# The channel weight of a mixer kernel loaded in full rows, and the first batches' steps placed anew

## The chip, the cores and the metric

The kernel runs on one core of one Trainium2 chip. The time is the device time of one execution in microseconds (us). The kernel before was run three times: 288.15, 288.61 and 289.21 us, so the median is 288.61 us. One execution of its own was profiled.

## The reference

For each of 8 batches and 8 heads (576 positions, 64 columns) the first part is attention under a mask: heads 0 to 3 see the last 32 positions, heads 4 to 7 see every fourth of the last 128. The second part is a mixer over the heads' joined output x (576 x 512):

```
scores = where(mask, q @ k.T / 8, -1e9);  attn = softmax(scores);  x = attn @ v   (heads side by side)
h = relu(x.T @ w_tok1) @ w_tok2          # w_tok1 576x256, w_tok2 256x576
u = x + h.T
out = u + relu(u @ w_ch1) @ w_ch2        # w_ch1 512x1536, w_ch2 1536x512
```

Inputs and output are float32; the kernel computes in fp16 with float32 sums.

## The kernel before

**Engines.** TensorE (PE) does all products and some transposes. ScalarE (ACT) and VectorE (DVE) empty its PSUM banks: exponentials, the scaling by the row sums, relu, the sums with x and u, and copies of transposed tiles. GpSimd (POOL) casts the loaded q, k and v to fp16, masks scores, and issues the DMAs of the weights, which cast from float32 to fp16 on the way. SyncE (SP) issues the loads of q, k and v, the DMA transposes of later batches and the stores.

**Order.** The program is written in the order in which each engine runs it; no scheduler changes that. Batch 0's attention, its h1 (the token product, `emit_h1`) and its u run first, alone (lines 888 to 970). Then, for each batch b, `gen_main(b)` (lines 747 to 814) yields pieces of the channel product: 12 blocks `gp_b_mb` of four 512-column matmuls each, over the four 128-row blocks cb of w_ch1, each followed by a relu into `gt`; then the second product `yp_b_s`, in pieces of six 256-column matmuls, whose sum with u is stored. `interleave` (line 816) runs this main line and counts its time by the number that each piece yields, and puts between its pieces the steps of the following batches, sorted by the times written for them. So during the main line of batch b the attention of batch b+1 is finished (`value_steps`, av), h1 and u of batch b+1 are made (`mix_steps`), and the scores of batch b+2 are begun. The lists with the times stand in lines 1006 to 1042.

**Weights.** w_ch1 lies in three tiles `w3[0..2]`, each of all 512 rows and 512 of the 1536 columns, so each row of a tile is 2 KB of the input. Its loads are issued by POOL: `load_w3(0)` (line 878) after the four casts of v's plain heads, `load_w3(1)` (line 881) after the two casts of `l_vd`, `load_w3(2)` (line 984) between the first casts of batch 1. Channel block mb reads tile mb // 4. Behind `load_w3(1)` on POOL stands the cast of `l_vx` into `vt` (line 882), which the value products of heads 4 to 7 of batch 0 read (line 611).

**Banks.** PSUM has eight banks: three called main, which gp and yp take in turn; two called sc (scores); three called fl for the rest. A bank is written anew when the instruction that read it last is done.

**Batch 1.** For each pair hp of heads, `transposes` turns c_q and c_k on PE; DVE or ACT copies the turned q into `qz` (line 102 or 100) and DVE the turned k into `kt` (line 314). The score matmuls (line 425, after line 423, which writes the mask into the bank) read both. POOL casts all of c_q and c_k of batch 1. Batch 2 has its own turning (`bare_steps`, k copied in line 385) and scores in pairs of half-height matmuls (line 510). u is turned by `emit_uT` (names tpu; line 673 and others), which takes fl banks.

Of the kernel before, what the change touches and what calls it, by code (L numbers as in the profile page):

```python
# [68 lines left out]
def kernel(  # L69
# [16 lines left out]
    def fixed(name, shape, dtype=FP16):  # L86
        return sb.tile(shape, dtype, tag=name, bufs=1, name=name)
# [16 lines left out]
    def relu(eng, out, in_):  # L104
        if eng is nc.scalar:
            nc.scalar.activation(out=out, in_=in_, func=AF.Relu)  # L106
        else:
            eng.tensor_scalar_max(out=out, in0=in_, scalar1=0.0)  # L108
# [510 lines left out]
    def emit_h1(b, jb, half, t):  # L619
        x = xn[b]  # L620
        j = slice(jb, DTOK, 2)
        c = slice(256 * half, 256 * half + 256)
        w = w1p if half else w1n
        p = bank("fl", 3, f"h1p_{b}_{jb}_{half}")[:, 0:256]
        nc.tensor.matmul(out=p, lhsT=w1t[b % 2][:, j], rhs=x[:, 4, c], start=True, stop=False)  # L625
        for s in range(4):
            nc.tensor.matmul(out=p, lhsT=w[:, s, j], rhs=x[:, s, c], start=False, stop=(s == 3))  # L627
        relu(nc.vector if jb and (b == 1 or (b == 0 and half)) else nc.scalar, t[:, c], p)

    def emit_u(b, s, h1):  # L630
        p = bank("fl", 3, f"up_{b}_{s}")
# [67 lines left out]
    def score_steps(b, t0, dt, offs=(0.0, 0.7, 2.0), places=None, lag=0.0):  # L699

        steps = []
        if twinned(b):
            for g in range(2):
                f = scores_twin(b, g)
                at = t0 + g * dt
                steps.append((at, 0.86, lambda f=f: next(f)))
                for i in range(7 if g else 9):
                    steps.append((at + lag * (i + 1), 0.0, lambda f=f: next(f)))
            return steps
        for hp in range(4):  # L710
            at, at_s = places[hp] if places else (t0 + hp * dt, t0 + hp * dt + dt)
            for nm in ("q", "k"):
                steps.append((at + 0.9 * (nm == "k"), 0.28, lambda nm=nm, hp=hp: transposes(b, nm, hp)))
# [33 lines left out]
    def gen_main(b):  # L747
# [2 lines left out]
        m0 = 640 * odd  # L750

        def w3_block(cb, mb):
            return w3[mb // 4][:, cb, mb % 4:512:4]

        def gp_tails(g):
            p = bank("main", 3, f"gt_{b}_{g}")
            for i in range(4):
                for cb in order:
# [3 lines left out]
            relu(nc.scalar, gta[:, 4 * g:4 * g + 4, 512:640],  # L762
                 p.rearrange("p (i t) -> p i t", t=128))

        for mb in range(NMB):
            p = bank("main", 3, f"gp_{b}_{mb}")
            for i, cb in enumerate(order):
                nc.tensor.matmul(out=p, lhsT=w3_block(cb, mb), rhs=uT[(b, cb)][0], start=(i == 0), stop=(i == 3))  # L768
                if i == 1:
                    yield 0.43  # L770
            relu(nc.vector if (mb % 2 == 1 if b == 0 else mb % 4 != 3 if b == 1 else mb in (1, 5)) else nc.scalar, gta[:, mb, m0:m0 + 512], p)
            yield 0.43
            if odd and mb in (3, 6, 9):
                gp_tails(mb // 3 - 1)
                yield 0.9
# [80 lines left out]
        nc.gpsimd.tensor_copy(out=t, in_=src)  # L856

    def load_w3(i):
        c = slice(512 * i, 512 * i + 512)
        nc.gpsimd.dma_start(out=w3[i], in_=moe_w_ch1[:, c].rearrange("(x p) c -> p x c", p=128))  # L860

    cast_qk(0, "q", 0, nc.scalar)
    cast_qk(0, "k", 0, nc.vector)
# [11 lines left out]
    for s in range(4):  # L875
        cast_vn(0, s, nc.gpsimd)
    nc.gpsimd.dma_start(out=w2a[:, :, 0:S], in_=moe_w_tok2.rearrange("(p j) t -> p j t", j=2))
    load_w3(0)
    cast_vd(0, 0, nc.gpsimd)
    cast_vd(0, 2, nc.gpsimd)  # L880
    load_w3(1)
    cast_vx(0, nc.gpsimd)
# [96 lines left out]
            load_qk(1, nm, h0, h0 + 4, nc.sync)  # L979
    load_v(1)  # L980
    casts1 = cast_steps(1)
    for i in (0, 1):
        casts1[i]()
    load_w3(2)
    for i in (2, 3, 4, 5, 7, 6, 8, 9, 10, 11):
        casts1[i]()
    for i in range(3):
        nc.gpsimd.dma_start(
# [17 lines left out]
    for b in range(B):  # L1006
        steps = []
        if b == 0:
            steps += score_steps(1, 0, 0, (0.0, 0.7, 1.5),
                                 ((3.0, 5.2), (4.4, 7.0), (7.2, 9.6), (8.6, 11.4)))  # L1010
            va = value_steps(1, 13.4, 0.7)
            steps += va[:4] + [(p + 0.3, c, f) for p, c, f in va[4:]]
            steps += mix_steps(1, 18.0, 20.6, 22.6, 31.4, 1.1)
            steps += at(24.0, 0.3, cast_steps(2))
            bare = bare_steps(2)
            scores2 = score_steps(2, 29.6, 4.4, lag=0.25)
            scores2 = sorted(scores2, key=lambda st: st[0])
            steps += [(t, 0.25, f) for t, f in zip((25.2, 25.9, 27.0, 27.6, 28.2, 34.8, 35.2, 35.6, 36.0), bare)]
            steps += scores2[:10]
            steps += at(34.0, 0.0, [lambda: emit_loads_qk(3)])  # L1020
        elif b == 1:
            va = value_steps(2, 0.0, 1.0)
            steps += [(0.8 + 0.4 * i, c, f) for i, (_, c, f) in enumerate(scores2[10:])]
            steps += [(t, c, f) for t, (_, c, f) in zip((2.2, 3.0, 4.8, 5.6, 8.2, 9.0, 10.4, 11.2), va)]
            steps += mix_steps(2, 7.0, 12.4, 14.6, 24.4, 1.0, 5.6, 0.8)
# [6 lines left out]
            steps += at(11.0, 0.9, dma_steps(3)) + at(17.0, 0.4, place_steps(3))  # L1032
        else:
            late = 2.4 * (b % 2)
            if b + 1 < B:
                steps += value_steps(b + 1, 0.4, 0.95) + mix_steps(b + 1, 5.4, 9.0, 11.4, 22.4 + late)
# [36 lines left out]
```

## Time and profile before

| | us |
|---|---|
| median of three runs | 288.61 |
| the profiled execution, its own time | 289.66 |
| span of that execution, first to last instruction | 287.8 |
| outside the span | 1.9 |
| PE busy | 276.8 |
| DVE, ACT, POOL busy | 132.1, 134.0, 163.0 |
| mean granted TensorE clock | 1.00 |

All times below are us from the start of the span. In a timeline row stand the start, the busy time, the engine, the line, the operation, the names written and read, the shape, and how many instructions the row merges; in brackets stands for how long the engine was idle before it and what ended that. The busy time of a matmul contains its way through the array, so matmuls that follow each other overlap: the time from one start to the next is what each costs. A wait shorter than that way leaves no bracket and shows only in the starts.

Batch 0's channel product starts at 28.47 and batch 1's at 69.24.

### The profile page before, as it was taken

To read this page: it belongs to the slowest core of one execution; us is meant where nothing else is said; L and a number is where in the kernel's file an instruction comes from. 1 tells how busy PE (TensorE), PEld (TensorE's weight loads), DVE (VectorE), ACT (ScalarE), POOL (GpSimd) and SP (SyncE) were. 2 spreads that over 40 slices of the span, in tenths; PEclk is the share of its full clock that TensorE was granted. 3 is DMA by queue.
4 is the path that set the end of the run, shared out by engine and by line. 5 is a ranking of instruction groups with operands and counts; after the bars stand their busy time and mean duration, and the time that the engine had idled before them with its cause. 6 is when DMAs were issued, how large, how long until landed. Compare 5 with 4: busy or idle time off the path is not lost.

```text
span 287.8 us, 6995 instructions
## 1 busy us (share of the span) xinstructions
PE 276.8 (96%) x2838; PEld 210.9 (73%) x2838; DVE 132.1 (46%) x278; ACT 134.0 (47%) x265; POOL 163.0 (57%) x221
## 2 busy tenths in 40 slices
PE   5879999999999999999999999999999999999995
PEld 2777676888766886698776976797766966886594
DVE  7747658446764236414640164416440274421022
ACT  2854673263543804574447615482546534225500
POOL 6961860478865799449970999279952930000000
PEclk9999999999999999999999999999999999999999
DMA  7999999993999998979888978299974210431023
GB/s 218 263 211 218 283 225 207 320 218 82 328 210 192 264 264 230 139 164 350 226 159 182 330 224 186 57 219 329 193 150 95 85 64 2 91 112 37 0 76 108
DMA packets 105551, 52.63 MB, mean 183 GB/s; under 512 B 73872, under 2 KB 104464, under 8 KB 105520
## 3 DMA queue, kind: packets, MB, share of 16 engines
q1 hardware_dynamic: 101280, 47.07, 67.0%
q0 software_dynamic: 2640, 3.94, 8.0%
q10 hardware_dynamic: 1600, 1.18, 1.4%
q8 instruction: 22, 0.36, 0.6%
q14 instruction: 9, 0.07, 0.1%
HBM read 37.07 MB, written 9.44 MB: 162 GB/s over the span
## 4 chain that ended last, share of the span: by engine, by line
PE 80%; DMA 8%; DVE 3%; POOL 3%; issue 2%; ACT 2%; ACTq 1%; SPq 0%; POOLq 0%; DVEq 0%
PE yp L787 29%; PE gp L768 24%; DMA l_vd<-in_v_dram 4%; PE h1p L627 4%; PE yp L807 3%; DMA l_k<-in_k_dram 3%; PE up L639 3%; PE sc L510 3%; PE gt L759 3%; DVE xn L112 1%; DMA kr<-c_k 1%; PE h1p L625 1%; PE av L608 1%; PE up L650 1%; PE av L603 1%
## 5 line engine op out<-in xcount | busy, mean ns | idle before, releaser
L787 PE MATMUL yp<-w,gt 128*128 128x256 f16 x756 | 87.1, 273 | 0.0
L787 PEld LDWEIGHTS <-gt 128*128 128x128 f16 x768 | 78.6, 106 | 6.5
L106 ACT ACTIVATE gt<-gp 128x512 f16<-128x512 f32 x69 | 41.2, 597 | 76.3 <-PE gp L768 76.0
L768 PE MATMUL gp<-utd,w 128*128 128x512 f16 x144 | 54.7, 380 | 0.0
L768 PE MATMUL gp<-utm,w 128*128 128x512 f16 x144 | 54.6, 379 | 0.0
L768 PEld LDWEIGHTS <-w 128*128 128x128 f16 x384 | 39.2, 114 | 20.3 <-issue 0.5
L797 DVE TENSOR_TENSOR o<-yp,u 128x512 f32<-128x512 f32 x31 | 21.4, 691 | 63.1 <-PE yp L787 58.5
L112 POOL TENSOR_TENSOR attp<-attp,const 128x1280 f16<-128x1280 f16 x12 | 31.4, 2616 | 27.5 <-ACT attp L534 27.4
L112 DVE TENSOR_TENSOR xn<-av,rec 128x320 f16<-128x320 f32 x64 | 31.4, 491 | 2.2
L112 POOL TENSOR_TENSOR attd<-attd,const 128x1024 f16<-128x1024 f16 x12 | 25.3, 2132 | 1.6 <-ACT attd L534 1.6
L768 PE MATMUL gp<-uT,w 128*128 128x512 f16 x96 | 25.8, 379 | 0.0
L108 DVE TENSOR_SCALAR gt<-gp 128x512 f16<-128x512 f32 x27 | 18.5, 686 | 13.6 <-PE gp L768 13.1
L645 DVE TENSOR_TENSOR u<-up,xn 128x512 f16<-128x512 f32 x26 | 17.9, 690 | 7.5 <-PE up L639 7.5
L534 ACT ACTIVATE attp<-sc 128x480 f16<-128x480 f32 (+1 forms) x36 | 16.1, 536 | 7.4 <-PE sc L510 7.4
L102 POOL CAST c_k<-l_k 128x512 f16<-128x512 f32 x29 | 18.0, 628 | 1.9 <-DMA l_k<-in_k_dram 1.7
L102 POOL CAST c_q<-l_q 128x512 f16<-128x512 f32 x27 | 16.8, 629 | 3.1 <-DMA l_q<-in_q_dram 3.1
L616 DVE RECIPROCAL rec<-av 128x5 f32<-128x5 f32 x64 | 12.2, 190 | 13.8 <-PE av L613 13.7
L106 ACT ACTIVATE h<-h1p 128x256 f16<-128x256 f32 x29 | 11.1, 384 | 14.5 <-PE h1p L627 14.1
L399 POOL COPY kt<-kr 128x512 f16<-128x512 f16 x10 | 10.7, 1075 | 9.0 <-DMA kr<-c_k 9.0
L697 ACT COPY utd<-utm 128x512 f16<-128x512 f16 x12 | 12.8, 1135 | 4.1 <-DMA utm<-u 4.1
L102 POOL CAST vv<-l_vn 128x256 f16<-128x256 f32 x32 | 12.0, 420 | 4.3 <-DMA l_vn<-in_v_dram 4.1
L112 POOL TENSOR_TENSOR attt<-attt,const 128x512 f16<-128x512 f16 x12 | 14.0, 1165 | 0.0
(147 smaller groups left out, 459.9 us busy)
## 6 DMA issues: line engine op xcount, KB each, us to landing
out_dram<-o SPq DMA_DIRECT2D x72, 128.0 KB, 3.1
l_q<-in_q_dram SPq DMA_DIRECT2D x15, 512.0 KB, 7.2
l_k<-in_k_dram SPq DMA_DIRECT2D x14, 512.0 KB, 7.1
l_vn<-in_v_dram SPq DMA_DIRECT2D x32, 128.0 KB, 6.6
l_vd<-in_v_dram SPq DMA_DIRECT2D x16, 256.0 KB, 4.6
w<-in_moe_w_ch_dram POOLq DMA_DIRECT2D x6, 512.0 KB, 7.6
lt<-in_q_dram SPq DMA_DIRECT2D x8, 128.0 KB, 4.6
l_vt<-in_v_dram SPq DMA_DIRECT2D x8, 128.0 KB, 4.9
```

Source lines behind the costliest of these rows:

```text
L102: eng.tensor_copy(out=out, in_=in_)
L106: nc.scalar.activation(out=out, in_=in_, func=AF.Relu)
L108: eng.tensor_scalar_max(out=out, in0=in_, scalar1=0.0)
L112: eng.tensor_tensor(out=out, in0=x, in1=y, op=ALU.mult)
L534: nc.scalar.activation(out=out, in_=in_, func=AF.Exp, scale=0.125)
L616: nc.vector.reciprocal(out=rec[:, :, 0], in_=av[:, :, 64])
L627: nc.tensor.matmul(out=p, lhsT=w[:, s, j], rhs=x[:, s, c], start=False, stop=(s == 3))
L645: nc.vector.tensor_tensor(out=u16(b, s), in0=blocks4(p), in1=blocks4(xn[b][:, s]), op=ALU.add)
L697: nc.scalar.copy(out=natural(uTd[:, cb - 2]), in_=uTm[i][:, cb].rearrange("p r m -> p m r"))
L768: nc.tensor.matmul(out=p, lhsT=w3_block(cb, mb), rhs=uT[(b, cb)][0], start=(i == 0), stop=(i == 3))
L787: nc.tensor.matmul(out=p[:, c], lhsT=gta[:, mb, a0:m0 + 512:4] if half else gta[:, mb, a0:a0 + 128], rhs=w4[mb][:, c], start=(mb == 0), st ...
L797: nc.vector.tensor_tensor(out=blocks4(o32), in0=blocks4(p), in1=u16(b, s), op=ALU.add)
```

## The change

- w_ch1 lies in two tiles of full rows: `w3[0]` holds row blocks cb 0 to 2 with all 1536 columns (6 KB of the input a row), `w3[1]` block cb 3. There are two loads; the third is gone from its place among batch 1's casts. On POOL the first load is issued after the first cast of `l_vd`, not before it.
- In batch 0, gp_0, gp_1 and gp_2 first run their matmuls over cb 0 to 2 in the three main banks; then their fourth matmuls run one after the other.
- c_q of batch 1's pairs 0 and 1 is cast by ACT, not POOL.
- Batch 1's transposes of q and of k have times of their own, and with their scores, values, h1 and u and with batch 2's first steps stand 1.0 to 1.6 later in the list of batch 0's main line.
- DVE no longer does the relu of gp_7, gp_9 and gp_11 of batch 0, and of batch 1's h1; ACT does.
- In batch 1's main line, h1's second half of batch 2 stands at 13.0, not 12.4, u at 15.1, not 14.6, and the placing of batch 3's turned k at 16.4, not 17.0. In odd main lines from 3 on h1 stands 0.4 later.

```
-    w3 = [fixed(f"w3_{i}", [128, 4, 512]) for i in range(3)]
+    w3 = [fixed(f"w3_{i}", [128, 3 - 2 * i, DCH]) for i in range(2)]
...
+            return w3[cb // 3][:, cb % 3, c0 + mb % 4:c0 + 512:4]
...
+        if b == 0:
+            for mb in range(3):
+                first.append(bank("main", 3, f"gp_{b}_{mb}"))
+                for cb in range(3):
+                    nc.tensor.matmul(out=first[mb], lhsT=w3_block(cb, mb), rhs=uT[(b, cb)][0], start=(cb == 0), stop=False)
+                yield 0.65
...
-                                 ((3.0, 5.2), (4.4, 7.0), (7.2, 9.6), (8.6, 11.4)))
-            va = value_steps(1, 13.4, 0.7)
+                                 ((4.2, 5.9, 7.1), (5.0, 6.6, 8.9), (7.8, 9.2, 11.2), (9.0, 10.2, 13.0)))
+            va = value_steps(1, 14.8, 0.7)
```

POOL in the program's start, before. `l_vd` and `l_vx` are loaded v, `vv` and `vt` their casts, `w_0` and `w_1` tiles of w_ch1.

```order
L877 DMA w_81<-in_moe_w_tok_dram 128x2x576
L860 DMA w_0_84<-in_moe_w_ch_dram 128x4x512
L102 CAST vv_69<-l_vd_123 128x4x2x64 x2
L860 DMA w_1_85<-in_moe_w_ch_dram 128x4x512
L102 CAST vt_71<-l_vx_124 128x4x64
```

POOL at the same place, now.

```order
L887 DMA w_81<-in_moe_w_tok_dram 128x2x576
L102 CAST vv_69<-l_vd_122 128x4x2x64
L869 DMA w_0_84<-in_moe_w_ch_dram 128x3x1536
L102 CAST vv_69<-l_vd_122 128x4x2x64
L869 DMA w_1_85<-in_moe_w_ch_dram 128x1536
L102 CAST vt_71<-l_vx_123 128x4x64
```

The first load moved behind one cast; the second still stands ahead of the cast into `vt`.

DVE in batch 0's main line, before. `tp_q_1` is the bank with the turned q of pair 1, and so on.

```order
L108 TENSOR_SCALAR gt<-gp_3_677 128x512
L314 COPY kt<-tp_k_0_695 128x512
L102 COPY qz<-tp_q_1_701 64x576 x2
L102 COPY kt<-tp_q_1_701 128x64
L314 COPY kt<-tp_k_1_724 128x512
L108 TENSOR_SCALAR gt<-gp_5_713 128x512
```

DVE at the same place, now.

```order
L108 TENSOR_SCALAR gt<-gp_3_673 128x512
L102 COPY qz<-tp_q_1_699 64x576 x2
L102 COPY kt<-tp_q_1_699 128x64
L108 TENSOR_SCALAR gt<-gp_5_696 128x512
L314 COPY kt<-tp_k_0_714 128x512
L314 COPY kt<-tp_k_1_723 128x512
```

The copy of pair 0's k, which the first scores of batch 1 read, moved behind the copies of pair 1's q and the relu of gp_5. On PE there stand between gp_4 and those scores, now: tp_q_0, half of gp_5, tp_q_1, the rest of gp_5, half of gp_6, tp_k_0, the rest of gp_6, tp_k_1.

DVE ahead of batch 2's first scores, before. `u_1` is u of batch 1, `o_0_1` an output tile, `kt` from `tp_k_1` the turned k of pair 1 of batch 2.

```order
L645 TENSOR_TENSOR u_1_1065<-up_3_1124,xn_886 128x4x128
L385 COPY kt<-tp_k_0_1131 128x512
L385 COPY kt<-tp_k_1_1153 128x512
L797 TENSOR_TENSOR o_0_1_1100<-yp_1_1099,u_0_499 128x512
L102 COPY uT_0_1240<-tpu_0_1239 128x640
```

DVE at the same place, now.

```order
L645 TENSOR_TENSOR u_1_1072<-up_3_1134,xn_893 128x4x128
L385 COPY kt<-tp_k_0_1142 128x512
L807 TENSOR_TENSOR o_0_1_1077<-yp_1_1076,u_0_498 128x512
L385 COPY kt<-tp_k_1_1167 128x512
L102 COPY uT_0_1244<-tpu_0_1243 128x640
```

The sum for the output tile moved ahead of the copy of k. On PE one piece of yp stands between these scores and the first turning of u (tpu_2), where two stood.

More of the change, by code (lines that the diff above doesn't have):

```diff
@@ L627, in emit_h1 @@
             nc.tensor.matmul(out=p, lhsT=w[:, s, j], rhs=x[:, s, c], start=False, stop=(s == 3))
-        relu(nc.vector if jb and (b == 1 or (b == 0 and half)) else nc.scalar, t[:, c], p)
+        relu(nc.vector if jb and half and b == 0 else nc.scalar, t[:, c], p)
     def emit_u(b, s, h1):
@@ L710, in score_steps @@
         for hp in range(4):
-            at, at_s = places[hp] if places else (t0 + hp * dt, t0 + hp * dt + dt)
-            for nm in ("q", "k"):
-                steps.append((at + 0.9 * (nm == "k"), 0.28, lambda nm=nm, hp=hp: transposes(b, nm, hp)))
+            at_q, at_k, at_s = places[hp] if places else (t0 + hp * dt, t0 + hp * dt + 0.9, t0 + hp * dt + dt)
+            for nm, at in (("q", at_q), ("k", at_k)):
+                steps.append((at, 0.28, lambda nm=nm, hp=hp: transposes(b, nm, hp)))
             g = (scores_plain if hp < 2 else scores_dil)(b, hp)
@@ L763, in gp_tails @@
                  p.rearrange("p (i t) -> p i t", t=128))
+        first = []
+        if b == 0:
[4 more added lines that the diff above has]
+                yield 0.65
         for mb in range(NMB):
-            p = bank("main", 3, f"gp_{b}_{mb}")
+            p = first[mb] if mb < len(first) else bank("main", 3, f"gp_{b}_{mb}")
             for i, cb in enumerate(order):
+                if mb < len(first) and i < 3:
+                    continue
                 nc.tensor.matmul(out=p, lhsT=w3_block(cb, mb), rhs=uT[(b, cb)][0], start=(i == 0), stop=(i == 3))
@@ L770, in gen_main @@
                     yield 0.43
-            relu(nc.vector if (mb % 2 == 1 if b == 0 else mb % 4 != 3 if b == 1 else mb in (1, 5)) else nc.scalar, gta[:, mb, m0:m0 + 512], p)
-            yield 0.43
+            relu(nc.vector if (mb % 2 == 1 and mb < 7 if b == 0 else mb % 4 != 3 if b == 1 else mb in (1, 5)) else nc.scalar, gta[:, mb, m0:m0 + 512], p)
+            yield 0.22 if mb < len(first) else 0.43
             if odd and mb in (3, 6, 9):
@@ L858, in load_w3 @@
     def load_w3(i):
-        c = slice(512 * i, 512 * i + 512)
-        nc.gpsimd.dma_start(out=w3[i], in_=moe_w_ch1[:, c].rearrange("(x p) c -> p x c", p=128))
+        nc.gpsimd.dma_start(
+            out=w3[i], in_=moe_w_ch1[384 * i:384 + 128 * i, :].rearrange("(x p) c -> p x c", p=128))
     cast_qk(0, "q", 0, nc.scalar)
@@ L877 @@
     nc.gpsimd.dma_start(out=w2a[:, :, 0:S], in_=moe_w_tok2.rearrange("(p j) t -> p j t", j=2))
+    cast_vd(0, 0, nc.gpsimd)
     load_w3(0)
-    cast_vd(0, 0, nc.gpsimd)
     cast_vd(0, 2, nc.gpsimd)
@@ L981 @@
     casts1 = cast_steps(1)
[L982 to L985, printed above, removed]
+    for i in (0, 2, 4, 5, 7, 6, 8, 9, 10, 11):
         casts1[i]()
@@ L1031 @@
             steps += at(6.0, 0.0, [lambda: load_v(3)]) + at(20.8, 0.9, load_steps(4))
-            steps += at(11.0, 0.9, dma_steps(3)) + at(17.0, 0.4, place_steps(3))
+            steps += at(11.0, 0.9, dma_steps(3)) + at(16.4, 0.4, place_steps(3))
         else:
@@ L1035 @@
             if b + 1 < B:
-                steps += value_steps(b + 1, 0.4, 0.95) + mix_steps(b + 1, 5.4, 9.0, 11.4, 22.4 + late)
+                steps += value_steps(b + 1, 0.4, 0.95) + mix_steps(b + 1, 5.4 + late / 6, 9.0, 11.4, 22.4 + late)
             if b + 2 < B:
```

15 lines of the change are left out of this document (8 added, 7 removed).

## Prediction

> **What bounds the kernel now.** The page of the profile first:
>
> ```profile
> span 287.8 us, 6995 instructions
> ...
> PE 276.8 (96%) x2838; PEld 210.9 (73%) x2838; DVE 132.1 (46%) x278; ACT 134.0 (47%) x265; POOL 163.0 (57%) x221
> ```
>
> PE is busy for 96% of the span. So time is made of PE's work, which the change leaves as it is (the same matmuls in another order), and of PE's waits. The page's own time was 289.66, 1.86 us more than the span; I sum against it and carry the difference to the median of the runs, 288.61, which is 1.05 lower. Next the list of what PE waited for, total, times, longest:
>
> ```profile
> PE av L611 <- POOL vt L102: 1.2, 1, 1.2
> ...
> PE h1p L625 <- DVE xn L112: 0.4, 1, 0.4
> ```
>
> Apart from the launch the first of these is PE's longest wait: the value products of batch 0 wait 1.2 us for `vt`. The others are small, so all that there is to win lies in that row and in stalls of about half a us; what there is to lose is any new wait on PE.
>
> **The front, POOL.** The timeline of POOL:
>
> ```profile
> 15.31 0.77 POOL L860 DMA_DIRECT2D w<-in_moe_w_ch_dram  x1
> 16.55 0.62 POOL L102 CAST vv<-l_vd 128x512 f16<-128x512 f32 x1 [0.46 <-DMA l_vd<-in_v_dram]
> 19.08 0.63 POOL L102 CAST vv<-l_vd 128x512 f16<-128x512 f32 x1 [1.91 <-DMA l_vd<-in_v_dram]
> 19.65 0.74 POOL L860 DMA_DIRECT2D w<-in_moe_w_ch_dram  x1
> 20.38 0.42 POOL L102 CAST vt<-l_vx 128x256 f16<-128x256 f32 x1
> ...
> 30.21 0.61 POOL L102 CAST c_q<-l_q 128x512 f16<-128x512 f32 x1 [0.80 <-DMA l_q<-in_q_dram]
> ...
> 39.20 1.61 POOL L988 DMA_DIRECT2D w<-in_moe_w_ch_dram  x3
> ```
>
> The weight's second load (19.65) takes 0.74 and stands between the second `l_vd` cast and the `vt` cast. It has 512 rows of 2 KB now and will have 128 of 6 KB; the loads at 39.20, 128 rows each, take 1.61 for three, 0.54 for one. So `vt` comes 0.20 earlier, and with it PE's start of the channel product: -0.20. The first load now goes into the 1.91 us in which POOL waits for `l_vd` at 17.2, at no cost to anyone. The bounds: 0, if an issue costs the same whatever its rows; -1.2, the whole wait, if `l_vd` lands sooner because the weight is not issued ahead of it. I take -0.20: the row 39.20 has just these 128 rows, and before 17.2 little of the weight can have moved. [...]
>
> **Does the weight arrive?** What POOL's DMA queue moved (packets, MB, share of the engines) from 19 to 24, all w_ch1 in packets of 1 KB, with the issue's time to landing, and from 42 to 48, w_ch2 in packets of 4 KB:
>
> ```profile
> q0 software_dynamic: 782, 0.79, 104.5%
> ...
> w<-in_moe_w_ch_dram POOLq DMA_DIRECT2D x1, 512.0 KB, 6.9
> ```
> ```profile
> q0 software_dynamic: 336, 1.25, 104.4%
> ```
>
> 0.79 MB in 5 us are 158 GB/s, 1.25 MB in 6 us 208. Rows of 3 KB in fp16 lie nearer to the second; I take 190. The first tile, 1.18 MB, then needs 6.2 us and the second, 0.39 MB, 2.1. Of the 6.9 to landing 3.3 were the moving of 0.52 MB and 3.6 the rest; so, issued at 17.2, the first is there at 27.0 and the second at 29.1. PE asks at 28.3 and 30.4 (below). The cover is 1.3; beyond it each us costs one.
>
> **Batch 0's channel product.** PE, and ACT with one later row:
>
> ```profile
> 28.47 3.48 PE L768 MATMUL gp<-uT,w 128*128 128x512 f16 x14
> 31.79 0.39 PE L309 MATMUL tp_q<-const,c_q 128*128 128x128 f16 x4
> ...
> 32.07 1.03 PE L768 MATMUL gp<-uT,w 128*128 128x512 f16 x4
> 32.93 0.39 PE L309 MATMUL tp_k<-const,c_k 128*128 128x128 f16 x4
> ```
> ```profile
> 28.45 0.59 ACT L100 COPY uT<-tpu 128x512 f16<-128x512 f16 x1 [0.38 <-PE tpu L673]
> 29.83 0.60 ACT L106 ACTIVATE gt<-gp 128x512 f16<-128x512 f32 x1 [0.79 <-PE gp L768]
> ...
> 81.26 1.13 ACT L100 CAST c_q<-l_q 128x512 f16<-128x512 f32 x2
> ```
>
> Four channel matmuls cost 32.93 - 32.07 = 0.86, so 0.215 each; five turnings 0.28. On the clock of before: nine matmuls from 28.47, with the short wait for the turned u that ACT ends at 29.04, reach 30.6. There gp_0's fourth starts; it is out 0.38 later (1.03 less three steps), and ACT's relu takes 0.60, so the bank is free at 31.6. PE has run the three fourths by 31.25 and waits for that bank with gp_3: +0.4 (0.3 to 0.5). No work covers it; in the order of before two whole blocks lie between. The wait of 0.1 for the last turned u goes.
>
> Then gp_3 to 32.5, gp_4 to 33.4, tp_q_0, half of gp_5, tp_q_1 to 34.4, and so on to the first scores at 36.1. The casts of c_q on ACT (1.13 for two, last row) follow the relu of gp_2 and end at about 33.3; tp_q_0 asks at 33.4. They start no sooner than q has landed, in the row of POOL at 30.21; the weight's longer load may push that back by 2, to 32.2, just in time.
>
> **The late copy.** DVE at this place:
>
> ```profile
> 32.70 0.69 DVE L108 TENSOR_SCALAR gt<-gp 128x512 f16<-128x512 f32 x1 [1.31 <-PE gp L768]
> 33.35 0.69 DVE L314 COPY kt<-tp_k 128x512 f16<-128x512 f16 x1
> 33.96 1.51 DVE L102 COPY qz<-tp_q 64x576 f16<-64x576 f16 x2
> 35.49 0.23 DVE L102 COPY kt<-tp_q 128x64 f16<-128x64 f16 x1
> 35.63 0.68 DVE L314 COPY kt<-tp_k 128x512 f16<-128x512 f16 x1
> ```
>
> Now tp_q_1 is out at 34.6. From there the two copies of q cost 1.53 (33.96 to 35.49), the small one 0.14, the relu of gp_5 0.60 to 0.65 (rows 32.70 and 35.63, to the next start), and the copy of pair 0's k 0.69: it ends at 37.5. PE reaches the first score that reads it at 36.2, and all of PE's later work is queued behind that matmul. I take +1.3. Lower bound 0.3: tp_k_0 leaves PE only at 35.5, so even a copy that nothing delayed would end at 36.4. Upper bound 1.7, if ACT's casts come late.
>
> Batch 1's scores, and its values with h1, by the view of windows (length, PE busy):
>
> ```profile
> 34.30:43.10 8.80, 8.46 (x127) 7.02 (x126) 5.90 (x13) 6.59 (x15) 6.33 (x14) 1.00 1.16 220
> 43.10:53.20 10.10, 9.90 (x119) 7.13 (x116) 7.47 (x21) 2.63 (x6) 0.91 (x3) 1.00 1.07 238
> ```
>
> PE idles 0.34 and 0.20 there. I leave that as it is: DVE has fewer relus, but u's first product now stands right behind h1's last, whose relu nothing covers. 0, between -0.5 and +0.3.
>
> **Before batch 2's scores.** PE, ACT and DVE:
>
> ```profile
> 61.19 1.50 PE L787 MATMUL yp<-w,gt 128*128 128x256 f16 x12
> 62.65 0.38 PE L673 MATMUL tpu<-const,u 128*128 128x128 f16 x4
> ...
> 69.24 0.59 PE L768 MATMUL gp<-uT,w 128*128 128x512 f16 x2
> ```
> ```profile
> 62.19 0.40 ACT L534 ACTIVATE attt<-sc 128x256 f16<-128x256 f32 x1
> ```
> ```profile
> 59.89 0.69 DVE L385 COPY kt<-tp_k 128x512 f16<-128x512 f16 x1 [0.35 <-PE tp_k L378]
> 62.07 0.69 DVE L797 TENSOR_TENSOR o<-yp,u 128x512 f32<-128x512 f32 x1 [1.49 <-PE yp L787]
> ```
>
> Twelve yp matmuls from 61.19 would end at 62.5; the turning of u starts at 62.65, just behind 62.60, when ACT has emptied the bank that it takes. Six of the twelve now stand ahead of the scores, so 0.65 of cover is gone: +0.65 (0.3 to 0.7). And the copy of k that the scores of pair 1 read (59.89, 0.69) now follows the sum for an output tile (0.69, 0.60 of it until the next can start). With yp's end as zero: PE is at those scores after a turning, six yp matmuls and the first scores (0.22 + 0.65 + 0.2 = 1.1); the copy ends after yp's way through the array, the sum and itself (0.25 + 0.60 + 0.69 = 1.55): +0.45 (0 to 0.5).
>
> **The later batches.** PE in the main lines of batches 1 and 3; that of batch 5 has the same wait as that of 3:
>
> ```profile
> 80.93 1.03 PE L768 MATMUL gp<-uT,w 128*128 128x512 f16 x4
> 82.35 0.28 PE L625 MATMUL h1p<-xn,w1t 128*128 128x256 f16 x1 [0.39 <-DVE xn L112]
> ```
> ```profile
> 140.28 0.19 PE L613 MATMUL av<-vv,attt 128*128 128x65 f16 x1
> 140.56 0.28 PE L625 MATMUL h1p<-xn,w1t 128*128 128x256 f16 x1
> ```
>
> In the first, four matmuls from 80.93 end at 81.79 and h1's second half starts at 82.35, 0.56 lost; two more channel matmuls now stand ahead of it. In the second, 0.25 are lost at 140.56; half a gp now stands there. Both stalls go, and 2 x 0.25 in batches 3 and 5 are kept. The 0.56 I count as lost again:
>
> ```profile
> 91.53 0.44 PE L510 MATMUL sc<-qt,kt 64*128 64x160 f16 x8 [0.21 <-POOL kt L399]
> ```
> ```profile
> 90.41 1.06 POOL L399 COPY kt<-kr 128x512 f16<-128x512 f16 x1
> ```
>
> The scores of batch 3 wait for POOL's copy of k, which ends at 91.47 and hangs on a DMA turning, whose place in SP's queue the change leaves; the move of that step to 16.4 changes nothing in POOL's order. PE comes 0.56 sooner and waits 0.56 longer. Bounds: -0.77 (that wait, 0.21, goes too) to 0.
>
> **Sum.** Front -0.20; batch 0: +0.4 - 0.1 + 1.3 + 0.65 + 0.45 = +2.7; later -0.5. In all +2.0: 291.66 for an execution like the profiled one, 290.6 as a median.
>
> **The rivals.**
> 1. The front gives the whole wait. Place: POOL's second `l_vd` cast; if its data lands before about 17.9, not 19.05, `vt` is no longer waited for, and -1.2 takes the place of -0.20: 289.6. For it: the weight's packets no longer stand between. Against: a load takes 6.9 from issue to landing, so the one issued at 15.31 can have moved little before 17.9.
> 2. The later gain stays. Place: POOL's copy of batch 3's k. If it ends 0.8 sooner against PE's clock, because PE is now later and the DMAs ahead of it in SP's queue are not: -0.77, so 289.8.
> 3. Not slower, but faster: DVE, freed of five relus, is ahead. Place: DVE's copy of pair 0's k; if it ends by 36.4 on the old clock, PE waits 0.3 there and not 1.3 (-1.0), batch 1's scores and values wait no more (-0.5), and before batch 2 the lower bounds hold (0.3 and 0, -0.8): 288.3, and with the gains of rivals 1 and 2 in full (-1.0, -0.77) 286.5. For it: DVE is idle for 1.3 ahead of the relu of gp_3 (row 32.70). Against: the order puts that copy last of five, and the one ahead of it, 1.53, cannot start before PE has turned pair 1's q.
> 4. The loads come late. [...] No run here shows 3 KB packets beside others.
>    As a mechanism of this kernel: q of batch 1 shares the engines with the weight's last 2 us; if it lands at 33.5 and not 32.2, PE waits 0.7 to 1.3 at tp_q_0, and if the second tile passes 30.4, as much again. 291.3 to 293.2.
>
> **How the numbers follow.** 0.5% is 1.44 us, about what a measurement can tell here, so faster means below 287.17 and slower above 290.05. Chances: forecast 0.43 (its own range 289.8 to 291.4; 0.04 of it below 290.05), rival 1 0.12, rival 2 0.17, rival 3 0.15 (0.12 of it faster), rival 4 0.13. Slower: 0.39 + 0.13 = 0.52. Same: 0.04 + 0.12 + 0.17 + 0.03 = 0.36. Faster 0.12. The range leaves out rival 3 below 287.5 (0.12) and the last of rival 4 (0.06): 287.5 to 292.4.
>
> **What would show it.** Right: PE waits at gp_3 for a relu on ACT (0.4), at the first scores of batch 1 for the copy of k on DVE (about 1.3), at the first turning of u for ACT (0.8); batch 1's channel product starts about 2.5 later than 69.24; the `vt` wait is near 1.0. Wrong: that start moves by less than 1, the copy of k is done before PE asks, or the wait for `vt` is gone.

## The result and the profile after

| | before | after |
|---|---|---|
| median of 17 runs each, us | 288.61 (287.77 to 289.38) | 290.29 (289.27 to 292.04) |
| ratio of the two, 95% interval | | 1.0069 (1.0052 to 1.0086) |
| the profiled execution's own time | 289.66 | 290.26 |

The changed kernel is slower by 0.7%, 1.7 us. First its page:

```profile
span 288.5 us, 6997 instructions
...
PE 277.3 (96%) x2838; PEld 211.0 (73%) x2838; DVE 130.6 (45%) x273; ACT 137.3 (48%) x272; POOL 161.1 (56%) x218
```

PE's busy time is again 96% of the span, on the same matmuls. So the difference lies in PE's waits, and these are the longest of them behind the launch (total, times, longest):

```profile
PE sc L425 <- DVE kt L314: 2.0, 3, 1.3
PE tpu L673 <- ACT attt L534: 0.6, 1, 0.6
PE tp_q L309 <- ACT c_q L100: 0.4, 1, 0.4
PE sc L510 <- DVE kt L385: 0.3, 1, 0.3
...
```

The wait for `vt` is gone. In its place stand the copies of k on DVE (2.0 in three waits for batch 1, 0.3 for batch 2), the first turning of u (0.6) and the cast of c_q on ACT (0.4). Where that puts the time is seen from the starts of the channel products on PE's timeline; a stage is the time from one product's start to the next one's:

| stage | before | after | difference |
|---|---|---|---|
| launch to batch 0's product | 28.47 | 27.01 | -1.46 |
| batch 0's main line | 40.77 | 44.33 | +3.56 |
| batch 1's main line | 35.82 | 34.88 | -0.94 |
| from there to the last matmul | 178.91 | 178.38 | -0.53 |

They add up to +0.63; the two executions differ by 0.60. The medians differ by 1.68. So about 1.1 us belongs to the profiled executions alone, and the experiments have to say to which stage.

**The front.** POOL now:

```profile
15.99 0.61 POOL L102 CAST vv<-l_vd 128x512 f16<-128x512 f32 x1 [0.71 <-DMA l_vd<-in_v_dram]
16.54 0.75 POOL L869 DMA_DIRECT2D w<-in_moe_w_ch_dram  x1
17.29 0.64 POOL L102 CAST vv<-l_vd 128x512 f16<-128x512 f32 x1
17.85 0.59 POOL L869 DMA_DIRECT2D w<-in_moe_w_ch_dram  x1
18.44 0.41 POOL L102 CAST vt<-l_vx 128x256 f16<-128x256 f32 x1
```

The second cast of `l_vd` starts at 17.29 without a wait (before: 19.08, after 1.91 of waiting), and `vt` is cast at 18.44. This is the event that the prediction put into rival 1. In this execution the product's start hangs on the weight: its first loading on PE (PEld) waits 0.19 for the first tile, so the cover that the prediction gave this load is gone.

```profile
27.00 1.66 PEld L771 LDWEIGHTS <-w 128*128 128x128 f16 x9 [0.19 <-DMA w<-in_moe_w_ch_dram]
```

Before, that loading, at 28.42, waits for no load, and PE's lists of waits in the six runs below with the old tiles have no row for the weight.

**Batch 0's channel product.** PE, and the weight load on PE that ends the one new wait in it:

```profile
27.01 2.13 PE L771 MATMUL gp<-uT,w 128*128 128x512 f16 x9
29.26 0.84 PE L778 MATMUL gp<-uT,w 128*128 128x512 f16 x3
30.35 1.89 PE L778 MATMUL gp<-uT,w 128*128 128x512 f16 x8 [0.25 <-ACT gt L106]
32.64 0.40 PE L309 MATMUL tp_q<-const,c_q 128*128 128x128 f16 x4 [0.40 <-ACT c_q L100]
...
36.93 0.24 PE L425 MATMUL sc<-qz,kt 128*128 128x160 f16 x1 [1.31 <-DVE kt L314]
```
```profile
29.25 0.58 PEld L778 LDWEIGHTS <-w 128*128 128x128 f16 x4 [0.60 <-DMA w<-in_moe_w_ch_dram]
```

The fourth matmuls wait for the weight's second tile, which lands at 29.25 (the weight load on PE was idle 0.60 for it; the nine matmuls before it, 0.216 from start to start, end their streaming 0.29 earlier). gp_3 starts 0.42 late at 30.35, behind gp_0's relu on ACT. tp_q_0 starts 0.57 late at 32.64, behind ACT's cast of c_q. The first score that reads k starts at 36.93, 1.48 late. ACT and DVE at these places:

```profile
31.97 1.14 ACT L100 CAST c_q<-l_q 128x512 f16<-128x512 f32 x2 [1.18 <-DMA l_q<-in_q_dram]
```
```profile
33.91 1.52 DVE L102 COPY qz<-tp_q 64x576 f16<-64x576 f16 x2 [1.81 <-PE tp_q L329]
35.45 0.23 DVE L102 COPY kt<-tp_q 128x64 f16<-128x64 f16 x1
35.59 0.68 DVE L108 TENSOR_SCALAR gt<-gp 128x512 f16<-128x512 f32 x1
36.19 1.28 DVE L314 COPY kt<-tp_k 128x512 f16<-128x512 f16 x2
```

q landed at 31.97, where ACT's cast starts, and the copy of pair 0's k stands behind qz1's two copies, the small one and the relu of gp_5: it is the first of the two at 36.19 and ends at 36.9. The list of steps explains the order: the turning of pair 0's k stands 2.0 later in it than before (5.9 for 3.9) and that of pair 1's q only 0.6 (5.0 for 4.4), not 1.0 to 1.6 as "The change" has it for all of them, so pair 1's q now comes first.

**Before batch 2's scores.** PE, ACT and DVE:

```profile
63.41 0.44 PE L510 MATMUL sc<-qt,kt 64*128 64x160 f16 x8 [0.27 <-DVE kt L385]
...
63.95 0.83 PE L797 MATMUL yp<-w,gt 128*128 128x256 f16 x6
65.41 0.38 PE L673 MATMUL tpu<-const,u 128*128 128x128 f16 x4 [0.63 <-ACT attt L534]
```
```profile
64.95 0.40 ACT L534 ACTIVATE attt<-sc 128x256 f16<-128x256 f32 x1
```
```profile
62.07 0.68 DVE L807 TENSOR_TENSOR o<-yp,u 128x512 f32<-128x512 f32 x1
62.67 0.68 DVE L385 COPY kt<-tp_k 128x512 f16<-128x512 f16 x1
```

The scores of pair 1 start 0.43 late at 63.41, since the copy at 62.67 stands behind the output sum at 62.07. The turning of u starts 0.79 late at 65.41; ACT's exponential at 64.95, which ends at 65.35, is the one that it waits for.

**The later main lines.** h1's second half of batch 2, batch 3's scores with POOL's second copy of k, and h1 in batch 3's main line:

```profile
83.03 1.89 PE L778 MATMUL gp<-uT,w 128*128 128x512 f16 x8
84.76 0.27 PE L625 MATMUL h1p<-xn,w1t 128*128 128x256 f16 x1
```
```profile
92.47 0.65 PE L510 MATMUL sc<-qt,kt 64*128 64x160 f16 x14
```
```profile
91.56 1.07 POOL L399 COPY kt<-kr 128x512 f16<-128x512 f16 x1
```
```profile
140.71 0.20 PE L613 MATMUL av<-vv,attt 128*128 128x65 f16 x1
140.74 0.27 PE L625 MATMUL h1p<-xn,w1t 128*128 128x256 f16 x1
```

After eight channel matmuls from 83.03 (1.73) h1 follows at 84.76 with no stall. The fourteen score matmuls from 92.47 run without a wait for k. h1 follows av directly at 140.74.

### The profile page after: what moved, and what is told of

Read it like the earlier page. It is cut to its first block, busy times and chain, and to the rows that moved or that the text cites. A ratio compares the mean times of both kernels' runs of the same rounds, so it can differ in the third digit from the quotient of the medians.

```text
span 288.5 us, 6997 instructions
## 1 busy us (share of the span) xinstructions
PE 277.3 (96%) x2838; PEld 211.0 (73%) x2838; DVE 130.6 (45%) x273; ACT 137.3 (48%) x272; POOL 161.1 (56%) x218
## 4 chain that ended last, share of the span: by engine, by line
PE 87%; DMA 5%; DVE 4%; ACT 1%; issue 1%; ACTq 0%; DVEq 0%; POOLq 0%
PE yp L797 28%; PE gp L778 27%; PE h1p L627 5%; PE up L639 4%; PE gt L760 4%; PE yp L817 4%; DMA l_q<-in_q_dram 3%; PE sc L510 3%; DMA const<-consts 2%; PE av L608 1%; PE av L603 1%; PE h1p L625 1%; PE sc L425 1%; DVE qz L102 1%; PE up L650 1%; PE av L601 1%
## 5 line engine op out<-in xcount | busy, mean ns | idle before, releaser
L106 ACT ACTIVATE gt<-gp 128x512 f16<-128x512 f32 x72 | 42.9, 597 | 73.7 <-PE gp L778 73.4
L778 PEld LDWEIGHTS <-w 128*128 128x128 f16 x375 | 38.0, 114 | 20.1 <-DMA w<-in_moe_w_ch_dram 0.6
L778 PE MATMUL gp<-uT,w 128*128 128x512 f16 x87 | 23.3, 380 | 0.4 <-ACT gt L106 0.3
L108 DVE TENSOR_SCALAR gt<-gp 128x512 f16<-128x512 f32 x24 | 16.5, 688 | 12.4 <-PE gp L778 11.8
L106 ACT ACTIVATE h<-h1p 128x256 f16<-128x256 f32 x31 | 11.9, 384 | 13.7 <-PE h1p L627 13.3
L399 POOL COPY kt<-kr 128x512 f16<-128x512 f16 x10 | 10.8, 1080 | 12.4 <-DMA kr<-c_k 12.4
L102 POOL CAST c_q<-l_q 128x512 f16<-128x512 f32 x25 | 15.6, 631 | 2.4 <-DMA l_q<-in_q_dram 2.1
L102 POOL CAST c_t<-lt 128x512 f16<-128x512 f32 x8 | 4.9, 618 | 15.4 <-DMA lt<-in_k_dram 15.4
## 6 DMA issues: line engine op xcount, KB each, us to landing
w<-in_moe_w_ch_dram POOLq DMA_DIRECT2D x1, 1152.0 KB, 10.4
```

The source lines that it names most:

```text
L102: eng.tensor_copy(out=out, in_=in_)
```

## The experiments

Theory A: the named waits of batch 0's main line are the whole cost; the long wait for `vt` belonged to one execution of the old kernel, so that the front is worth little; and of the later gain a part is lost again unless PE comes late to batch 3's scores. Theory B: the wait for `vt` is in every execution, and the change takes all of it away. Medians are given with the ratio to the kernel before, run on the same chip; "stage" is batch 0's main line as above (before 40.77, after 44.33).

### The weight in full rows alone

```
+    w3 = [fixed(f"w3_{i}", [128, 3 - 2 * i, DCH]) for i in range(2)]
...
+            for mb in range(3):
+                first.append(bank("main", 3, f"gp_{b}_{mb}"))
...
+    cast_vd(0, 0, nc.gpsimd)
     load_w3(0)
-    cast_vd(0, 0, nc.gpsimd)
```

> The kernel before with the weight in full rows alone: two tiles, the first load behind the first cast of l_vd, three banks held open for gp_0 to gp_2; every step of the later batches stays where it was. Theory A (the front is worth little in a usual execution, since the 1.2 us wait for vt was long in the one profiled execution only): the front gives 0.2 to 0.4; the held banks cost about 0.5 (in the trace after, 0.29 at the fourth matmuls and 0.42 at gp_3, less 0.2 of waits that before had there): 288.7 (288.2 to 289.2) against 288.6 for the kernel before. Theory B (the wait for vt is there in each execution and the change takes it away): -1.4 + 0.5, so 287.7 (287.3 to 288.1). In the trace both expect no wait of PE for vt above 0.3 us; A expects other executions of the old front to show a shorter wait for vt too.

Measured 291.64, ratio 1.0110 (1.0072 to 1.0148); product start 27.16, stage 45.50. Both theories missed: neither had seen that q lands late (POOL's first cast of it, which waits for the load, starts at 32.30, before at 30.21). PE, then the windows around that place (length, PE busy with count, then the other engines; the third number from the end is the granted clock):

```profile
32.97 0.40 PE L309 MATMUL tp_q<-const,c_q 128*128 128x128 f16 x4 [1.89 <-POOL c_q L102]
```
```profile
31.00:34.50 3.50, 1.43 (x11) 0.67 (x11) 0.61 (x1) 0.97 (x2) 1.90 (x4) 1.00 1.09 347
34.50:37.90 3.40, 3.40 (x18) 2.07 (x19) 2.51 (x5) 1.10 (x3) 3.26 (x7) 0.50 1.14 235
```

PE waited 1.89 for POOL's cast of c_q, 2.05 from stream to stream, and then ran 3.4 us at half the clock, which cost 1.7. This happened in two of the six runs only: 292.74 and 293.49 had a mean clock of 0.993 and 0.994, the other four 0.999 or 1.000 and times from 290.48 to 292.08, their middle at 291.0. Without the slow clock too, then, the run lies 2.5 above the kernel before. So the new places of the turnings and the casts on ACT, which cost time themselves, hide most of a delay that the weight's load brings (1.89 of waiting for c_q here, 0.40 in the changed kernel); without them the weight costs more than the whole change.

### The same, with PE kept busy in that wait

```
+        if b == 1 and nm == "q" and hp == 0:
+            fill = bank("fl", 3, "idle_q")
+            for _ in range(8):
+                nc.tensor.matmul(out=fill, lhsT=idle[:, 0:128], rhs=idle, start=True, stop=True)
```

> The run with the weight in full rows alone, and eight products of zeros into a spare bank (0.215 us each, 1.72 in all, nothing reads them) ahead of the first turning of batch 1's q, where PE stood idle for 1.89 us. In that run the matmuls from 34.5 to 37.9 took twice their time, at a granted clock of 0.5. Theory A (the clock falls because PE stood idle): it stays at 1.00 now, the 1.65 us of slow matmuls are saved, and the time is 290.0 (289.5 to 290.5). Rival (the clock fell for another reason, and the idle time is no part of it): no gain, 291.6 (291.0 to 292.2).

Measured 290.52, ratio 1.0068 (1.0049 to 1.0086), 0.02 above A's range; stage 43.24, 2.26 shorter than without the filling. The same windows:

```profile
31.00:34.50 3.50, 3.34 (x26) 1.84 (x25) 1.24 (x2) 1.48 (x3) 2.31 (x5) 1.00 1.11 340
34.50:37.90 3.40, 3.30 (x43) 2.66 (x42) 2.42 (x5) 2.44 (x6) 3.23 (x8) 1.00 1.15 210
```

The clock stayed at 1.00 and PE did 43 matmuls in the 3.4 us in which it had done 18. The 2.26 are the 1.7 of slow matmuls and about 0.5 because the turning of q started sooner after the product's start (32.35, right behind the products of zeros; q's cast had ended at 31.9). All six runs had a mean clock of 0.998 or more. Against the four runs without the filling that kept their clock (middle 291.0) the gain is 0.5, and none fell here against two of six there: this fits theory A, but six runs of each don't show that the filling is what kept the clock.

### The later main lines alone

```
-            steps += mix_steps(2, 7.0, 12.4, 14.6, 24.4, 1.0, 5.6, 0.8)
+            steps += mix_steps(2, 7.0, 13.0, 15.1, 24.6, 1.0, 5.6, 0.8)
...
-                steps += value_steps(b + 1, 0.4, 0.95) + mix_steps(b + 1, 5.4, 9.0, 11.4, 22.4 + late)
+                steps += value_steps(b + 1, 0.4, 0.95) + mix_steps(b + 1, 5.4 + late / 6, 9.0, 11.4, 22.4 + late)
```

> The kernel before with the edits of the later main lines alone (batch 1: h1's second half, u and the placing of k; from batch 3 on: h1 0.4 later). Theory A (the forecast: the 0.56 at 82.35 is given back at batch 3's first scores, because POOL's copy of k keeps its time and PE comes sooner; the 0.25 of batches 3 and 5 are kept): -0.5, so 288.1 (287.8 to 288.4), and in the trace PE waits 0.7 to 1.0 us there for kt from line 399. Rival (nothing is given back, as in the trace after): -0.56 - 0.37 - 0.26 - 0.26 = -1.4, so 287.2 (286.9 to 287.5), and no wait for line 399.

Measured 287.53, ratio 0.9972 (0.9953 to 0.9991): faster than both kernels. Batch 1's main line took 35.56, 0.26 less than before, and the rest 178.39, 0.52 less. PE at batch 3's scores, and POOL:

```profile
90.11 0.44 PE L510 MATMUL sc<-qt,kt 64*128 64x160 f16 x8 [0.51 <-POOL kt L399]
```
```profile
89.00 1.05 POOL L399 COPY kt<-kr 128x512 f16<-128x512 f16 x1
```

The copy ends at 90.05 and the scores start at 90.11, 0.67 late from stream to stream, 0.30 more than before: about half of h1's 0.56 is given back, as the forecast had it in whole, and the rest is kept. The time lies between the two theories. This execution has the old front too, and POOL there shows no wait for `l_vd`:

```profile
15.35 0.77 POOL L860 DMA_DIRECT2D w<-in_moe_w_ch_dram  x1
16.11 1.34 POOL L102 CAST vv<-l_vd 128x512 f16<-128x512 f32 x2
17.39 0.74 POOL L860 DMA_DIRECT2D w<-in_moe_w_ch_dram  x1
18.90 0.41 POOL L102 CAST vt<-l_vx 128x256 f16<-128x256 f32 x1 [0.77 <-DMA l_vx<-in_v_dram]
```

Both casts of `l_vd` run at 16.11, `vt` is cast at 18.90, and PE's list of waits has no row for `vt`. The product starts at 27.33.

### Batch 3's scores one piece later

```
-            steps += score_steps(3, 21.0, 4.6, lag=0.1)
+            steps += score_steps(3, 21.65, 4.6, lag=0.1)
```

(on top of the later main lines alone)

> The run with the edits of the later main lines alone, and batch 3's scores one piece of yp (0.86) later. Theory A (of the 0.56 of h1's stall 0.30 was given back in the wait of 0.67 for POOL's copy of k, which keeps its time): that wait goes, 0.5 (0.3 to 0.67) less than that run's 287.5: 287.0 (286.8 to 287.3). Rival (the wait only moves, to the copy of the next pair or to batch 3's values): 287.5 (287.3 to 287.8).

Measured 287.42, ratio 0.9950 (0.9933 to 0.9967). Batch 1's main line took 34.88, 0.68 less than 35.56, and the wait is gone from PE's list. The median lies in the rival's range: this one is 1.26 below its kernel before, the run above 0.95 below its own, and the intervals overlap. By the trace theory A holds; the times alone would not tell it from the rival.

### The new places alone

```
+            steps += at(3.7, 0.0, [lambda hp=hp: cast_qk(1, "q", hp, nc.scalar) for hp in range(2)])
...
-                                 ((3.0, 5.2), (4.4, 7.0), (7.2, 9.6), (8.6, 11.4)))
+                                 ((4.2, 5.9, 7.1), (5.0, 6.6, 8.9), (7.8, 9.2, 11.2), (9.0, 10.2, 13.0)))
```

(with the later times of values, h1, u and batch 2's first steps, and the relus; weight and later main lines as before)

> The kernel before with the new places of batch 0's main line alone (batch 1's turnings, scores, values, h1 and u and batch 2's first steps later; c_q of pairs 0 and 1 cast by ACT; five relus moved from DVE to ACT); the weight in three tiles, no banks held, later main lines as before. Theory A (the places cost it, the held banks little): PE waits about 1.3 for the copy of k of pair 0, 0.7 to 0.8 at the first turning of u, about 1 in all at the scores and h1; 3.5 less 0.5 for the held banks, less 0.2 to 0.4 because PE now comes late enough to batch 3's scores: 291.2 (290.6 to 291.7). Rival C (what costs is that the banks are held and everything behind comes late, the places only +1): 289.6 (289.2 to 290.1), and the wait for the copy of k is under 0.6.

Measured 290.42, ratio 1.0060 (1.0034 to 1.0087); stage 43.50, +2.73. PE at the two places:

```profile
37.57 0.24 PE L425 MATMUL sc<-qz,kt 128*128 128x160 f16 x1 [1.31 <-DVE kt L314]
```
```profile
66.25 0.38 PE L673 MATMUL tpu<-const,u 128*128 128x128 f16 x4 [1.39 <-ACT attt L534]
```

The copy of k costs the same 1.48 (1.31 in the row) without any held bank, and c_q is not waited for. At the turning of u the wait is 1.55, for here no piece of yp stands between the scores and it. Rival C falls. The median is 0.2 below A's range; the ratio's interval reaches 291.0, inside it.

### The copy of k ahead of one relu

```
+            if b == 0 and mb == 5:
+                late_relu = lambda p=p, mb=mb: relu(nc.vector, gta[:, mb, m0:m0 + 512], p)
```

(called behind the copy of pair 0's k; all else as in the changed kernel)

> The changed kernel with one instruction moved: DVE's relu of gp_5 behind the copy of pair 0's k, not ahead of it. Theory A (PE's first scores of batch 1 wait for that copy and nothing else): the wait of 1.48 becomes about 0.85, and the time is 0.6 lower than the changed kernel's 290.3: 289.7 (289.3 to 290.0). Rival D (something else is late right behind it, the copy of pair 1's k or the bank of gp_5 for gp_8): the wait moves on, 290.3 (290.0 to 290.6).

Measured 289.41, ratio 1.0039 (1.0014 to 1.0063) against the changed kernel's 1.0069; stage 43.50, 0.83 less. PE and DVE:

```profile
35.90 0.24 PE L425 MATMUL sc<-qz,kt 128*128 128x160 f16 x1 [0.71 <-DVE kt L314]
```
```profile
35.16 0.68 DVE L314 COPY kt<-tp_k 128x512 f16<-128x512 f16 x1
35.76 0.68 DVE L108 TENSOR_SCALAR gt<-gp 128x512 f16<-128x512 f32 x1
```

The copy stands at 35.16, ahead of the relu at 35.76, and the wait is 0.88, not 1.48: one relu of 0.60 on another engine's queue was 0.60 of the kernel's time. The rest of the 0.83 are shorter waits in this execution for the weight's second tile (0.13 less) and for c_q (0.07 less).

### More cover ahead of u's turning

```
-            steps += mix_steps(1, 19.0, 21.6, 23.6, 32.4, 1.1)
+            steps += mix_steps(1, 19.0, 21.6, 23.6, 33.1, 1.1)
```

> The changed kernel with u's turnings of batch 1 0.7 later in the list, so that two pieces of yp stand again between batch 2's scores and the first turning, as in the kernel before. Theory A (PE waits there for ACT because half its cover is gone): the 0.79 at that place goes to under 0.2, the time is 0.6 to 0.7 below the changed kernel's 290.3: 289.6 (289.2 to 289.9). Rival (the turnings now come late for the channel product of batch 1): PE waits there for the last turned u instead, 290.2 (289.9 to 290.6).

Measured 289.51, ratio 1.0037 (1.0021 to 1.0053); stage 43.51, 0.82 less; the stall at the turning is 0.14, not 0.79. Theory A holds. (The rest is the weight's second tile, which is there in time when PE starts so late, less 0.15 more at c_q.) The profiled execution of this kernel, at 291.47 its slowest run, shows something else, at the product's start:

```profile
29.03 1.27 PE L771 MATMUL gp<-uT,w 128*128 128x512 f16 x5 [2.02 <-DMA w<-in_moe_w_ch_dram]
```

PE waited 2.02 for the weight's first tile, which landed 12.7 us after its issue and not 10.4 as in the changed kernel's profile, though the issue was no later (16.33 and 16.54). All of the cover that the prediction gave the load is used up, and the landing is the start.

### The changed kernel with the old weight

> The changed kernel with its weight as before: three column tiles, the old order on POOL, no banks held; the new places and the later edits stay. Theory A (the front is worth 0.3 to 0.5; the weight in full rows costs 0.7 at the held banks and 0.57 because q lands late): 0.8 below the changed kernel's 290.3: 289.5 (289.0 to 289.9). Theory B (the whole wait for vt of 1.3 was the change's gain): 290.3 + 1.4 - 1.3, so not below 290.3 (290.1 to 290.8).

(the edit is the first diff the other way round, with the third load back among batch 1's casts)

Measured 289.65, ratio 1.0043 (1.0024 to 1.0063); product start 26.83, stage 43.50. This lies in theory A's range, and the front agrees: with the old tiles and the old order on POOL the product starts at 26.83, no later than the 27.01 of the changed kernel, and the time is 0.6 lower. Four more profiles of the old front start it at 27.33, 27.96, 26.93 and 26.79, and a fifth, of the places alone, at 28.68, where PE waited 2.1 at the launch, until 8.00; none of the six has a wait for `vt`. The one with 28.47 is the exception, and the prediction was built on it. Of the 1.0 that the weight costs at the product's start in the trace (held banks and c_q), about 0.2 comes back here: without the held banks u's first turning waits 1.55, where the changed kernel waits 0.43 and 0.79 at the scores and the turning.

The ratio's intervals of this run and the two before it reach up to or past the 1.0052 at which the changed kernel's begins. The medians alone would not show these gains; they rest on the waits in the traces.

### The places mended

The old weight, the relu behind the copy, the later turnings of u, and batch 3's scores one piece later, all together.

> The changed kernel without the weight's part (three column tiles, no banks held), with DVE's relu of gp_5 behind the copy of pair 0's k, with two pieces of yp ahead of u's turnings, and with batch 3's scores one piece of yp later. Theory A (the new places cost what the named waits show, and nothing else): from the 289.6 of the run without the weight's part, 0.60 less at the copy of k and 1.4 less at u's first turning (1.55 there), so 287.6 (287.3 to 288.1): what is left of the new places is the rest of that wait, 0.9, against the kernel with the later edits alone. Rival (the places are late throughout, and a wait that is taken away comes back at the next place): not below 288.6 (288.6 to 289.4).

Measured 288.13, ratio 0.9992 (0.9975 to 1.0010): no difference from the kernel before, 0.03 above A's range, and clear of the run without the weight's part (1.0024 to 1.0063); stage 42.25. One size was missed, at u's first turning.

```profile
63.89 0.38 PE L673 MATMUL tpu<-const,u 128*128 128x128 f16 x4 [0.61 <-ACT attt L534]
```

Of the 1.55 there 0.78 went, for the 0.7 in the list puts one piece of yp ahead of it, and two are needed. With 0.60 + 0.78 the sum would have been 288.3. What was taken away did not come back elsewhere (the stage is 1.25 shorter, for 0.60 + 0.78), so the rival falls.

### Five relus from DVE to ACT, in the old order

```
-        relu(nc.vector if jb and (b == 1 or (b == 0 and half)) else nc.scalar, t[:, c], p)
+        relu(nc.vector if jb and half and b == 0 else nc.scalar, t[:, c], p)
...
-            relu(nc.vector if (mb % 2 == 1 if b == 0
+            relu(nc.vector if (mb % 2 == 1 and mb < 7 if b == 0
```

(on top of batch 3's scores one piece later)

> The run with the later edits and batch 3's scores later (287.4), with the five relus of batch 0's channel product and batch 1's h1 on ACT, not DVE, and nothing else of the change. Theory A (these relus are hidden on either engine; DVE has them behind the late copies, not ahead of them): no difference, 287.4 (287.1 to 287.7). Rival 3 of the forecast (DVE freed of them is ahead, and batch 1's values and h1 wait less): 0.3 to 0.8 less, 286.9 (286.6 to 287.1).

Measured 287.03, ratio 0.9948 (0.9927 to 0.9968); stage 40.60, against 41.03 and 40.75 in the two runs with the relus on DVE. That is a gain of 0.15 to 0.4 in the trace, and the median's difference from the run without it (1.52 against 1.26 below the kernel before) lies within the intervals. The median lies in rival 3's range, just outside A's. Not settled; a gain, if it is one, is under 0.5. This version has the lowest median of all: 1.5 us below the kernel before, 3.3 below the changed one.

## Why the prediction came out as it did

The time, 290.29, lies 0.3 from the forecast of 290.6, and batch 0's mechanism is as described. Two other terms were wrong, and it was luck that they and the missing part of batch 0 cancelled. Of the prediction's own signs the three waits came (0.42, 1.48, 0.79), and batch 1's product starts 2.1 later, for about 2.5; but so did one of its signs of being wrong: the wait for `vt` is gone.

**Batch 0's main line: +2.7 forecast, +3.56 measured.** By terms, in stalls of PE from stream to stream, after less before:

| term | forecast | measured |
|---|---|---|
| held banks: gp_3 behind ACT's relu +0.42, second weight tile +0.29, old waits at the start -0.30 | +0.3 | +0.41 |
| tp_q_0 behind ACT's cast of c_q | 0 | +0.57 |
| first scores of batch 1 behind DVE's copy of k | +1.3 | +1.48 |
| other scores, values, h1, u of batch 1 | 0 | 0.0 |
| scores of pair 1 of batch 2 behind the same engine's sum | +0.45 | +0.43 |
| first turning of u behind ACT (0.79, before 0.12) | +0.65 | +0.67 |

All three waits that the order alone gave away are there with their size; the experiments that undo two of them give back 0.60 and 0.65 at their places in the trace. Missed is c_q. The landings were right in this execution (the tiles at 27.0 and 29.25 for 27.0 and 29.1, q at 31.97 for 32.2), the first by two errors that cancel: it was issued at 16.54, not 17.2, and took 10.4, not 9.8. The time at which PE asks was wrong. With the front 1.46 earlier the cover of 1.3 was gone, and PE stood at tp_q_0 before q's cast was done. This is the mechanism of rival 4 in a small size.

**The front: -0.20 forecast.** The step that failed is not the 0.20 but its base: "the value products of batch 0 wait 1.2 us for `vt`" was taken as a property of the kernel. It was one of that execution, whose own time lay 1.05 above the median; the text carried the 1.05 to the median as a difference of unknown place, and then also let the wait stand in the kernel. Profile against profile the front gives 1.46; in six other executions of the old front the wait does not occur, and the change gains nothing there. What held the second half of `l_vd` back in the one execution is not settled. So rival 1 came true in the trace and not in the median.

**The later batches: -0.5 forecast, -1.47 measured.** The step that failed is "the 0.56 I count as lost again". Rival 2 had the reason: POOL's copy, against PE's clock, came sooner, because PE was late and the DMAs that it hangs on were less so. Batch 1's product started 2.10 later than before; the DMA turning that POOL's copies wait for was issued in SP's queue 1.2 later (85.61 and 86.77). The copy that batch 3's scores wait for ended 22.2 us after batch 1's product started before, and 21.3 after it now. The run without PE's lateness gives 0.30 back, so the later gain is worth 0.8 in itself and 1.5 in a kernel that has lost 2 us earlier. The 0.25 in batches 3 and 5 are gained wherever the edit is.

**What the change bought and paid.** The load in full rows bought nothing that an ordinary execution lacked. It did not make the weight faster either: the 158 GB/s from which the forecast went are a mean over five us of which one moved only 0.08 MB. In the run with the old weight rows of 1 KB moved 0.19 to 0.21 MB in each us from 19 to 23, those of 3 KB now 0.20 to 0.21 from 20 to 26. The load delays q (its first cast starts at 31.97, before at 30.21), and PE pays for the new order that hides this. By medians, each against the kernel before run beside it: 0.7 for the weight (1.68 less 0.97), 1.9 for the places (the run that has them alone), less 0.95 for the later main lines. That is 1.7, what was measured.

## What to carry to other kernels

A wait in one profile is a term of a sum only if the kernel's other executions have it: where the profiled run lies above the median by about the size of its longest wait, that wait is the first suspect, and a second profile settles it. When steps are moved to hide a late transfer, read on the other engines what now stands ahead of the copy that PE will ask for; here the order of two queues gave three waits to within 0.2 us. And gains behind a place where two chains meet depend on which is late: 0.56 of PE's stall was worth half of it until PE was made late elsewhere.

## What the runs showed of the hardware

**Batch 1's loads came behind the weight's, which are in another queue.** Rows that moved in each us, of the weight's loads (POOL's queue) and of batch 1's (SP's queue, issued from 21.18 in the run with the old weight and from 21.30 in the changed kernel):

| us | old weight, rows of 1 KB: weight, SP | rows of 3 KB: weight, SP |
|---|---|---|
| 21.5 to 22.5 | 204, 0 | 76, 0 |
| 22.5 to 23.5 | 206, 0 | 61, 0 |
| 23.5 to 24.5 | 107, 514 | 68, 0 |
| 24.5 to 25.5 | 33, 498 | 80, 3 |
| 25.5 to 26.5 | 7, 356 | 70, 56 |
| 26.5 to 27.5 | 0, 304 | 87, 682 |

With either length SP's rows move when the weight's get few (the 87 in the last line are 0.07 MB, against 0.18 to 0.23 in each us above), and the loads of 128 KB took 6.1 from issue to landing there and 8.4 and 8.8 here. The profile of the kernel before, with rows of 1 KB too, has the same turn: 193 rows and 0 from 23.5 to 24.5, 116 and 581 in the next us; its two loads of 128 KB took 5.2. What is sure to differ is how much lies ahead: two tiles, 1.05 MB, with the old weight, for the third is issued later, and all 1.57 MB now. The 0.52 MB more are 2.6 us at the 0.2 MB a us above, and by landing the two loads of 128 KB are 2.3 and 2.7 later. No run here has longer rows with as many bytes ahead, so the share of the row length stays open.

**Half the clock after about two idle microseconds, in some executions.** In the profiled run with the weight alone PE stood still for 1.89 and then had a granted clock of 0.50 for 3.4 us. In that of the places alone, after 2.1 us at the launch, the clock was 0.50 from 9.5 to 11.0. But after the 2.02 of the run with more cover the clock stayed at 1.00, and after the changed kernel's wait of 1.48 too. 3.4 us at half the clock take 0.006 off a run's mean clock; by that mark (0.993 or 0.994) it happened in two of six runs of the weight alone, in one of ten of the places alone and in none of six with the products of zeros; but also in one of 12 with the copy of k ahead of one relu and in one of 25 of the kernel before, two runs of which no profile shows whether PE had such a gap. So gaps of about the same length were followed by the slow stretch at one time and not at another; what decides it, no run here shows.
